# Weight splitting moved from GpSimd to VectorE, narrowing without a clamp, and a later check of the exponents

## The chip, the cores and the metric

One Trainium2 chip, one core. The metric is the device time of the slowest core (here the only one) in microseconds, for one execution of the whole program. Engines: PE (TensorE, with PEld for its weight loads), DVE (VectorE), ACT (ScalarE), POOL (GpSimd) and SP, whose queue issues most DMAs.

## The reference, cut to what matters

Three layers over 3072 tokens of 384 numbers: a recurrent attention, a layer of eight experts with a skip, and a gated layer. The last layer's weights come as 64-bit words (w_gate, w_val, w_out are float64).

```python
def _moe_ref(x, w_skip, w_gate, w1, w2):
    ...
        h = np.maximum(xc[mask] @ w1[e], 0.0)
        y[mask] = gate_w[mask, None] * (h @ w2[e])
    out[do_compute] = xc + y

def _moe2_ref(x, w_gate, w_val, w_out, rms_g):
    rms = np.sqrt(np.mean(x * x, axis=-1, keepdims=True) + 1e-06)
    xn = x / rms * rms_g
    g = xn @ w_gate
    silu = g * (1.0 / (1.0 + np.exp(-g)))
    val = xn @ w_val
    return (silu * val @ w_out).astype(np.float32)
```

w_gate and w_val have 384 x 1536 numbers, w_out 1536 x 384.

## The kernel before, in words

The program runs as one stream of three parts. The order of the instructions on each engine is fixed when the program is built: the build goes through the code in order, takes that order as priority, and places each instruction by a time model of its own. Each engine then works through its own list in that fixed order, and waits at an instruction whose inputs, or whose output buffer, are not ready. So an instruction that waits also holds all that stands behind it on its engine.

**Attention (0 to some 175 us of the profile)**: 24 tiles of 128 tokens, then routing: every token's row is scattered to a slot of its expert.

**Experts (to some 337 us)**: for each of 8 experts, `expert(e)` loads its 256 rows transposed, multiplies by w1 (`products`, line 993), takes relu over as a high and a low half (`relu`, hh on ACT at line 996, hl on DVE at 997) and multiplies by w2 (line 1040). All numbers that PE sees are split in two fp16 halves, hi and lo, and each product is three matmuls (hi hi, hi lo, lo hi). Beside the main loop run side jobs, as generators that are advanced by `steps`, a few steps after each piece of the main loop: `prep1` and `prep2` load and split the weights of an expert three ahead (`split`, lines 390 and 391); `place`, `first` and `middle` take rows of x, form the mean of squares and its inverse root (`square`, lines 444 to 458), and either scatter the normalised row to the buffer xnd (line 477) or transpose it into xnT (line 498).

**The gated layer (the rest)**: six blocks of 512 tokens. `up` makes, for one of 12 slices of 128 columns, the products pwg and pwv (line 846, 9 matmuls each), takes silu of pwg (sg, ACT, line 850), multiplies by pwv (hf, DVE, 852), and splits hf in gh (ACT, 855) and gl (DVE, 856). `down` multiplies these by w_out into four sums po (line 869, 12 matmuls). Blocks 0 and 1 run as one `pair`: all their `up` steps first, alternating, over four pairs of PSUM banks; then the `down` steps. Blocks 2 to 5 run by `block`, where `down` of slice m-1 follows `up` of slice m, over two pairs of banks. `later` brings in a later block's rows, by transposing DMAs on SP's queue.

Before `up` can use slice m it needs the weights of piece m // 2: `prep_in` for w_gate and w_val (6 pieces each of 384 x 256), `prep_out` for w_out (6 of 256 x 384). Each loads a piece as pairs of 32-bit words into a staging tile st (768 KB, four of them) and narrows each 64-bit float to a 32-bit one in `narrow`: the absolute value of the high word on ACT (line 190), a clamp to the range of exponents that the bit trick can take (DVE, 192), shift and mask (193), then sign (195) and low bits (197), all on DVE over 768 columns. The clamp lets a number outside that range show as a too small or too large one. For w_gate and w_val, `prep_in` then scales by rms_g on ACT (three instructions, line 409), casts to the hi half on ACT (414), and subtracts on POOL for the lo half (416). The narrowed tile fb has two buffers.

At the end, `bounds` (lines 916 to 949) gathers checks on ranges, with two small matmuls, and `last` makes a flag of them; if it is set, the program runs a slow general version instead. It is not set here.

Of the kernel before, what the change touches and what calls it, by code (L numbers as in the profile page):

```python
# [34 lines left out]
NPRE = 0  # L35
POOL_LO = True
WB = 3
# [8 lines left out]
N4 = 2  # L46
N5 = 1
HB = 24
FB = 2
# [34 lines left out]
def fused_kernel(ctx, tc, q, k, v, f, w_skip, w_gate, w1, w2, g_gate, g_val, g_out, rms_g, out, dbg=None):  # L84
# [48 lines left out]
    cnt = keep.tile([128, 2 * E + 1], F16, name="cnt")  # L133
    osum = keep.tile([128, NT], F32, name="osum")
    big = keep.tile([128, 2 + 2 * E + 3], F32, name="big")

# [49 lines left out]

    def narrow(o, lo, hi):


        nc.scalar.activation(out=o.bitcast(F32), in_=hi.bitcast(F32), func=AF.Abs)  # L190
        yield
        nc.vector.tensor_scalar(out=o.bitcast(F32), in0=o.bitcast(F32), scalar1=2.0 ** -15 * 1.125, scalar2=2.0 ** 16 * 1.9375, op0=ALU.max, op1=ALU.min)
        nc.vector.tensor_scalar(out=o, in0=o, scalar1=3, scalar2=0x3FFFFFFF, op0=ALU.logical_shift_left, op1=ALU.bitwise_and)
        yield
        nc.vector.scalar_tensor_tensor(out=o, in0=hi, scalar=-0x40000000, in1=o, op0=ALU.bitwise_and, op1=ALU.bitwise_or)
        yield
        nc.vector.scalar_tensor_tensor(out=o, in0=lo, scalar=29, in1=o, op0=ALU.logical_shift_right, op1=ALU.bitwise_or)
        yield
# [195 lines left out]
    def raw(src, n, wide):  # L394
        st = stg.tile([128, n, wide, 2], I32, tag="st", name="st64")
        load(st, src)
        yield
        fb = stg.tile([128, n, wide], I32, tag="fb", name="fb", bufs=FB)
        yield from narrow(fb, st[:, :, :, 0], st[:, :, :, 1])
        return fb.bitcast(F32)  # L400

    def prep_in(nm, p):
        src = (g_gate if nm == "wg" else g_val).bitcast(I32)
        wide = F2 // 6
        w = yield from raw(src[:, 2 * p * wide:2 * (p + 1) * wide].rearrange("(k p) (f t) -> p k f t", p=128, t=2), KD, wide)
        hi, lo = gT[nm][p]
# [15 lines left out]
    def prep_out(p):  # L422
        src = g_out.bitcast(I32)
        w = yield from raw(src[p * 256:(p + 1) * 256, :].rearrange("(k p) (d t) -> p k d t", p=128, t=2), 2, DM)
        yield from split(oT[p][0], oT[p][1], w, SO, 1)
        if p == 0:
            top(big[:, 2 + 2 * E + 2:3 + 2 * E + 2], oT[0][0][:, 0, 0:64])
# [12 lines left out]
    def square(xr, idx, y=None):  # L440
# [9 lines left out]
        m = nk.tile([128, 3], F32, tag="m2", name="m2", bufs=4)  # L450
        nc.scalar.activation(out=junk, in_=x2, func=AF.Square, accum_out=m[:, 0:1])
        nc.gpsimd.tensor_scalar(out=m[:, 1:2], in0=m[:, 0:1], scalar1=1.0 / DM, scalar2=1e-6 * SX * SX, op0=ALU.mult, op1=ALU.add)
        nc.gpsimd.tensor_tensor(out=m[:, 2:3], in0=m[:, 1:2], in1=mhalf[:, 0:1], op=ALU.pow)
# [8 lines left out]
    def place(xr, idx, y=None):  # L462
# [3 lines left out]
        if y is None:  # L466
            ms = m[:, 0:1]
        else:
            junk = nk.tile([128, DM], F32, tag="junk", name="junk", bufs=1)
            m3 = nk.tile([128, 1], F32, tag="m3", name="m3")  # L470
            nc.scalar.activation(out=junk, in_=parts(xr)[:, 0, :], func=AF.Square, accum_out=m3)
            ms = m3
# [358 lines left out]

    hs2 = {}

    def up(blk, m, b0):
# [20 lines left out]
        nc.scalar.copy(out=hh, in_=hf)  # L855
        nc.vector.tensor_tensor(out=hl, in0=hf, in1=hh, op=ALU.subtract)  # L856
        hs2[blk, m] = hh, hl
# [57 lines left out]
    def bounds():  # L915
        NBIG = 2 + 2 * E + 3
        NC = 3 + NBIG
        NA = NC + 2 * E + 1
        bad = keep.tile([128, NC], F32, name="bad")
        vio = keep.tile([128, 4], F32, name="vio")  # L920
        tot = keep.tile([1, NA + NT], F32, name="tot")
# [7 lines left out]
        worst(1, ex_sum, ALU.is_le, EXPSUM, ALU.max)  # L929
        worst(2, ms_x, ALU.is_ge, 1.0, ALU.min)  # L930
        nc.vector.tensor_scalar(out=bad[:, 3:NC], in0=big, scalar1=TINY, scalar2=None, op0=ALU.is_ge)
        pt = ps.tile([128, 512], F32, **bank(3), name="tot")
# [12 lines left out]

        beyond(0, 3, 127.5)
        beyond(3, NC, 0.5)
        beyond(NC, NC + E, LOW, CAP)
# [150 lines left out]
    with m1x:  # L1099
        for e in range(E):  # L1100
            need("a", e)
            need("e", e)
            run(expert(e), N2)
            if e + WB < E:
                add(prep1(e + WB), ("a", e + WB))
                add(prep2(e + WB), ("e", e + WB))
            if e < MID:
                add(middle(e), ("mid", e), 1)
            if 2 <= e < 6:
                for t in (0, 1):  # L1110
                    a = 2 * (e - 2) + t
                    add(first(a // NB, a % NB), ("b", a // NB), 1)
# [10 lines left out]
    for e in range(E):  # L1123
        need("y", e)
    later(2)
    for blk in range(2, NT // NB):
        if blk == NT // NB - 1:
            checks = bounds()
        for m, _ in enumerate(block(blk)):
            if m == 4 and blk + 1 < NT // NB:  # L1130
                later(blk + 1)

    fctx.close()
# [38 lines left out]
```

## Time and profile before

| | us |
|---|---|
| median of 3 runs | 774.69 (773.26 to 774.88) |
| profiled execution, its own time | 774.52 |
| its span | 772.8 |
| PE busy | 719.5 (93% of the span) |
| DVE busy | 417.7 (54%) |
| ACT busy | 362.7 (47%) |
| POOL busy | 216.1 (28%) |

The span is what the profile covers, 1.7 us less than the execution's time. Busy shares are means over three parts that differ; the rows further down are by stretch. The mean granted clock of PE was 0.977 of full speed.

### The profile page before, as it was taken

To read this page: it belongs to the slowest core of one execution; us is meant where nothing else is said; L and a number is where in the kernel's file an instruction comes from. 1 tells how busy PE (TensorE), PEld (TensorE's weight loads), DVE (VectorE), ACT (ScalarE), POOL (GpSimd) and SP (SyncE) were. 2 spreads that over 40 slices of the span, in tenths; PEclk is the share of its full clock that TensorE was granted. 3 is DMA by queue.
4 is the path that set the end of the run, shared out by engine and by line. 5 is a ranking of instruction groups with operands and counts; after the bars stand their busy time and mean duration, and the time that the engine had idled before them with its cause. 6 is when DMAs were issued, how large, how long until landed. Compare 5 with 4: busy or idle time off the path is not lost.

```text
span 772.8 us, 14043 instructions
## 1 busy us (share of the span) xinstructions
PE 719.5 (93%) x5452; PEld 442.8 (57%) x5452; DVE 417.7 (54%) x879; ACT 362.7 (47%) x803; POOL 216.1 (28%) x286
## 2 busy tenths in 40 slices
PE   8999798995999888769999999999999999999995
PEld 5788687784776655534444566455455455555443
DVE  2788386885688888999999700222222222222230
ACT  5887477643577667778766410222312222123131
POOL 5221742442165565677320010200100020002002
PEclk9999899997999999999999999999999999999998
DMA  9999887844778998754332400100200030001001
GB/s 153 178 198 198 209 160 182 231 142 131 217 250 241 265 263 259 237 154 150 110 123 82 82 22 20 42 1 1 62 20 1 1 83 0 1 1 42 1 0 46
DMA packets 166459, 88.10 MB, mean 114 GB/s; under 512 B 137432, under 2 KB 151048, under 8 KB 166384
## 3 DMA queue, kind: packets, MB, share of 16 engines
q1 hardware_dynamic: 161904, 74.44, 39.9%
q0 software_dynamic: 4480, 12.67, 4.5%
q8 instruction: 45, 0.74, 0.4%
q14 instruction: 30, 0.25, 0.1%
HBM read 64.18 MB, written 16.24 MB: 104 GB/s over the span
## 4 chain that ended last, share of the span: by engine, by line
PE 67%; DVE 9%; DMA 8%; ACT 5%; POOL 4%; issue 4%; SPq 2%; POOLq 0%; ACTq 0%; DVEq 0%
PE po L869 18%; PE pwv L846 18%; PE pwg L846 18%; DMA st<-in_moe_w_dram 3%; PE py L641 2%; DMA xnd<-xn,at 2%; PE sc L625 2%; DVE w2l L391 2%; SPq L557 1%; PE py L636 1%; DVE w1l L391 1%; PE ptq L607 1%; DVE xn L458 1%; DVE hl L997 1%; DMA st<-in_moe_w_gate_dram 1%
## 5 line engine op out<-in xcount | busy, mean ns | idle before, releaser
L852 DVE SCALAR_TENSOR_TENSOR hf<-pwv,sg 128x512 f32<-128x512 f32 x72 | 49.5, 689 | 181.4 <-PE pwv L846 181.4
L877 POOL DMA_INDIRECT out_dram<-ot,ids x24 | 23.7, 988 | 336.8 <-ACT ot L876 332.3
L846 PE MATMUL pwg<-xnT,wgh 128*128 128x512 f16 x432 | 106.3, 382 | 7.5 <-ACT sg L850 7.5
L846 PE MATMUL pwv<-xnT,wvh 128*128 128x512 f16 x432 | 105.6, 379 | 0.0
L855 ACT CAST gh<-hf 128x512 f16<-128x512 f32 x72 | 44.3, 615 | 108.5 <-DVE hf L852 108.3
L869 PE MATMUL po<-wol,gh 128*128 128x384 f16 x288 | 93.7, 326 | 0.0
L869 PE MATMUL po<-woh,gh 128*128 128x384 f16 x288 | 93.7, 326 | 0.0
L869 PE MATMUL po<-woh,gl 128*128 128x384 f16 x288 | 93.4, 326 | 0.0
L850 ACT ACTIVATE sg<-pwg 128x512 f32<-128x512 f32 x72 | 42.5, 593 | 101.4 <-PE pwg L846 101.4
L869 PEld LDWEIGHTS <-gh 128*128 128x128 f16 x576 | 56.4, 98 | 41.8
L846 PEld LDWEIGHTS <-wgh 128*128 128x128 f16 x432 | 42.5, 98 | 55.4 <-issue 8.9
L856 DVE TENSOR_TENSOR gl<-hf,gh 128x512 f16<-128x512 f32 x72 | 52.6, 731 | 35.4 <-ACT gh L855 35.4
L846 PEld LDWEIGHTS <-wvh 128*128 128x128 f16 x432 | 42.3, 98 | 50.4 <-issue 0.3
L993 PE MATMUL ph<-exT,w1h 128*128 128x256 f16 (+1 forms) x384 | 57.3, 276 | 8.5 <-DMA exT<-xs 8.5
L846 PE MATMUL pwg<-xnT,wgl 128*128 128x512 f16 x216 | 59.3, 381 | 0.0
L846 PE MATMUL pwv<-xnT,wvl 128*128 128x512 f16 x216 | 58.7, 379 | 0.0
L993 PEld LDWEIGHTS <-w1h 128*128 128x128 f16 x432 | 40.6, 101 | 19.9 <-DMA exT<-xs 8.6
L1040 PE MATMUL ey<-w2h,hh 128*128 128x384 f16 x112 | 37.0, 331 | 7.1 <-ACT hh L996 7.1
L588 POOL TENSOR_TENSOR qs<-q,ep 128x384 f32<-128x384 f32 x24 | 26.8, 1117 | 56.3 <-ACT ep L584 38.5
L876 ACT ACTIVATE ot<-po 128x384 f32<-128x384 f32 x24 | 11.6, 489 | 58.2 <-PE po L869 50.9
L869 PEld LDWEIGHTS <-gl 128*128 128x128 f16 x288 | 28.2, 98 | 18.6
L1040 PE MATMUL ey<-w2h,hl 128*128 128x384 f16 x112 | 31.4, 332 | 7.1 <-DVE hl L997 5.2
(203 smaller groups left out, 1396.0 us busy)
## 6 DMA issues: line engine op xcount, KB each, us to landing
st<-in_moe_w_dram SPq DMA_DIRECT2D x32, 768.0 KB, 6.3
f<-in_f_logit_dram SPq DMA_DIRECT2D x24, 192.0 KB, 4.6
q<-in_q_dram SPq DMA_DIRECT2D x24, 192.0 KB, 4.0
k<-in_k_dram SPq DMA_DIRECT2D x24, 192.0 KB, 4.6
v<-in_v_dram SPq DMA_DIRECT2D x24, 192.0 KB, 4.4
st<-in_moe_w_gate_dram SPq DMA_DIRECT2D x6, 768.0 KB, 4.6
st<-in_moe_w_val_dram SPq DMA_DIRECT2D x6, 768.0 KB, 4.6
st<-in_moe_w_out_dram SPq DMA_DIRECT2D x6, 768.0 KB, 4.3
```

The source lines that it names most:

```text
L391: nc.vector.scalar_tensor_tensor(out=lo[:, :, sl], in0=src[:, :, sl], scalar=scale, in1=hi[:, :, sl], op0=ALU.mult, op1=ALU.subtract)
L588: nc.gpsimd.tensor_tensor(out=qs[:, :, 0:D], in0=ins["q"], in1=ep, op=ALU.mult)
L625: nc.tensor.matmul(scs[r][:, j, :], lhsT=T["k"][64 * r:64 * r + 64, j, :], rhs=T["q"][64 * r:64 * r + 64, j, :], start=True, stop=True)
L846: nc.tensor.matmul(p, lhsT=w, rhs=x, start=(j == 0), stop=(j == len(terms) - 1))
L850: nc.scalar.activation(out=sg, in_=pg, func=AF.Silu, scale=1.0 / SG)
L852: nc.vector.scalar_tensor_tensor(out=hf, in0=pv, scalar=SH / SG, in1=sg, op0=ALU.mult, op1=ALU.mult)
L855: nc.scalar.copy(out=hh, in_=hf)
L856: nc.vector.tensor_tensor(out=hl, in0=hf, in1=hh, op=ALU.subtract)
L869: nc.tensor.matmul(po[t], lhsT=a[:, sl], rhs=w, start=(m == 0 and j == 0), stop=(m == KF2 - 1 and j == 2))
L877: sc = nc.gpsimd.indirect_dma_start(out=out, out_offset=bass.IndirectOffsetOnAxis(ap=at[:, t:t + 1].bitcast(U32), axis=0), in_=ot, in_offs ...
L993: nc.tensor.matmul(out[:, i, :], lhsT=a, rhs=r, start=(j == 0), stop=(j == len(terms) - 1))
L1040: nc.tensor.matmul(py[t], lhsT=a[:, sl], rhs=w[:, m, :], start=(m == 0 and j == 0), stop=(m == KF - 1 and j == 2))
```

## The change

- `prep_in`: ACT's scaling writes the hi half directly (the cast is gone), and the lo half is made on DVE, by three instructions of 256 columns that scale and subtract, in place of one on POOL of 768.
- `narrow` without the clamp for these weights: neither the absolute value on ACT nor the clamp on DVE; the shift reads the raw high words in the staging tile. The side job of a piece of w_out is one step shorter for it; that of w_gate or w_val two, since the subtraction's own step is gone too.
- The range of exponents, which the clamp covered, is checked by `ranges`: each of the 18 pieces is loaded a second time, its exponent fields are shifted out, and their maximum and minimum are kept (DVE). It runs as a side job in the blocks from 2 on, two steps after each slice, behind gl on DVE, and must be over when the last block starts. `bounds` has two more columns.
- In `square` and `place` the mean's factor goes into ACT's scale, and the addition of epsilon moves from POOL to DVE.
- The table of functions that silu needs is loaded behind the last relu of expert 0, and not where silu is first met.

```diff
-POOL_LO = True
+POOL_LO = False
...
+N6 = 2
...
-    def narrow(o, lo, hi):
-        nc.scalar.activation(out=o.bitcast(F32), in_=hi.bitcast(F32), func=AF.Abs)
-        yield
-        nc.vector.tensor_scalar(out=o.bitcast(F32), in0=o.bitcast(F32), scalar1=2.0 ** -15 * 1.125, scalar2=2.0 ** 16 * 1.9375, op0=ALU.max, op1=ALU.min)
-        nc.vector.tensor_scalar(out=o, in0=o, scalar1=3, scalar2=0x3FFFFFFF, op0=ALU.logical_shift_left, op1=ALU.bitwise_and)
+    def narrow(o, lo, hi, clamp=True):
+        src = hi
+        if clamp:
+            nc.scalar.activation(out=o.bitcast(F32), in_=hi.bitcast(F32), func=AF.Abs)
+            yield
+            nc.vector.tensor_scalar(out=o.bitcast(F32), in0=o.bitcast(F32), scalar1=2.0 ** -15 * 1.125, scalar2=2.0 ** 16 * 1.9375, op0=ALU.max, op1=ALU.min)
+            src = o
+        nc.vector.tensor_scalar(out=o, in0=src, scalar1=3, scalar2=0x3FFFFFFF, op0=ALU.logical_shift_left, op1=ALU.bitwise_and)
...
-        yield from narrow(fb, st[:, :, :, 0], st[:, :, :, 1])
+        yield from narrow(fb, st[:, :, :, 0], st[:, :, :, 1], clamp=False)
...
+    def ranges():
+        j = 0
+        for source, n, wide in [in_source(nm, p) for nm in ("wg", "wv") for p in range(6)] + [out_source(p) for p in range(6)]:
+            st = stg.tile([128, n, wide, 2], I32, tag="st", name="st64")
+            nc.sync.dma_start(out=st, in_=source)
+            yield
+            fb = stg.tile([128, n, wide], I32, tag="fb", name="fb", bufs=FB)
+            nc.vector.tensor_scalar(out=fb, in0=st[:, :, :, 1], scalar1=20, scalar2=0x7FF, op0=ALU.logical_shift_right, op1=ALU.bitwise_and)
+            yield
+            nc.vector.tensor_reduce(out=expo[:, 0, j:j + 1], in_=fb, axis=AX.XY, op=ALU.max)
+            yield
+            nc.vector.tensor_reduce(out=expo[:, 1, j:j + 1], in_=fb, axis=AX.XY, op=ALU.min)
+            yield
+            j += 1
...
-        nc.scalar.activation(out=junk, in_=x2, func=AF.Square, accum_out=m[:, 0:1])
-        nc.gpsimd.tensor_scalar(out=m[:, 1:2], in0=m[:, 0:1], scalar1=1.0 / DM, scalar2=1e-6 * SX * SX, op0=ALU.mult, op1=ALU.add)
+        nc.scalar.activation(out=junk, in_=x2, func=AF.Square, scale=DM ** -0.5, accum_out=m[:, 0:1])
+        nc.vector.tensor_scalar(out=m[:, 1:2], in0=m[:, 0:1], scalar1=1e-6 * SX * SX, scalar2=None, op0=ALU.add)
...
-        nc.vector.tensor_tensor(out=hl, in0=hf, in1=hh, op=ALU.subtract)
+        gated.append(nc.vector.tensor_tensor(out=hl, in0=hf, in1=hh, op=ALU.subtract).ins)
...
+        worst(3, expo[:, 0], ALU.is_le, 1150.0, ALU.max)
+        worst(4, expo[:, 1], ALU.is_ge, 897.0, ALU.min)
...
+            if e == 0:
+                with tc.issue_after(pins[-1][0]):
+                    nc.scalar.preload_act_table_set("silu_and_others")
...
+    add(ranges(), ("ranges",))
     for blk in range(2, NT // NB):
         if blk == NT // NB - 1:
+            need("ranges")
             checks = bounds()
         for m, _ in enumerate(block(blk)):
             if m == 4 and blk + 1 < NT // NB:
                 later(blk + 1)
+            with tc.issue_after(gated[-1]):
+                steps(N6)
```

With `POOL_LO = False` the branch of `prep_in` that was not taken before is taken:

```python
            else:
                nc.scalar.activation(out=hi[:, j, :], in_=w[:, j, :], func=AF.Copy, scale=gsc[:, j:j + 1])
                nc.vector.scalar_tensor_tensor(out=lo[:, j, :], in0=w[:, j, :], scalar=gsc[:, j:j + 1], in1=hi[:, j, :], op0=ALU.mult, op1=ALU.subtract)
```

`issue_after(x)` places what stands in it behind x in the list of x's engine, without a wait.

## Rows read from the trace of the kernel before

**Rows 1.** Busy time by stretch of the span. Columns: the stretch in us and its length; then for PE, PEld (weight loads), DVE (VectorE), ACT (ScalarE) and POOL (GpSimd) the busy us in it and (x instructions); then the granted TensorE clock as a share of full speed, the DMA share and GB/s.
```profile
280.00:300.00 20.00, 16.38 (x112) 11.27 (x111) 13.76 (x33) 12.23 (x32) 9.88 (x12) 0.91 0.92 231
...
320.00:340.00 20.00, 17.31 (x107) 10.33 (x108) 19.92 (x32) 13.73 (x33) 16.97 (x15) 1.00 0.77 253
340.00:345.00 5.00, 0.00 (x0) 0.00 (x0) 4.93 (x12) 2.75 (x6) 3.46 (x5) 0.90 0.16 18
...
370.00:436.00 66.00, 66.00 (x307) 29.91 (x306) 63.40 (x85) 40.95 (x70) 10.62 (x6) 1.00 0.30 90
...
484.00:560.00 76.00, 76.00 (x389) 37.95 (x388) 18.06 (x27) 18.40 (x37) 5.61 (x6) 1.00 0.10 26
...
705.00:773.00 68.00, 58.89 (x307) 29.76 (x305) 14.39 (x23) 13.76 (x27) 3.88 (x4) 0.96 0.04 14
```

**Rows 2.** Instructions of PE in order of time at the start of the last part. Columns: start us, length us (of the whole group), engine, line, operation, output<-inputs, shape, how many; in brackets the idle time before and what ended it.
```profile
339.09 0.81 PE L846 MATMUL pwg<-xnT,wgl 128*128 128x512 f16 x3
347.44 2.72 PE L846 MATMUL pwg<-xnT,wgh 128*128 128x512 f16 x6 [7.53 <-ACT sg L850]
349.95 1.26 PE L846 MATMUL pwg<-xnT,wgl 128*128 128x512 f16 x3
...
352.99 1.46 PE L846 MATMUL pwg<-xnT,wgh 128*128 128x512 f16 x6
```

**Rows 3.** The chain of waits that ended last, in order of time, between 311 and 348 us. Columns: start us, us that the piece adds to the chain, engine, tile and line.
```profile
317.97 0.86 DVE w2l L391
...
320.65 0.47 DVE fb L192
...
321.64 0.33 DVE hl L997
...
328.94 0.88 DVE fb L197
...
338.52 1.60 POOL wgl L416
...
340.14 0.92 ACT fb L190
...
342.12 0.07 DVE at L476
...
345.49 1.28 ACT L850
...
346.79 0.61 ACT sg L850
```

**Rows 4.** Instructions of DVE in order of time before the first gate product is taken over, columns as in rows 2.
```profile
324.30 1.99 DVE L458 SCALAR_TENSOR_TENSOR xn<-x,m,xn 128x384 f16<-128x384 f32 x1
...
334.23 1.54 DVE L458 SCALAR_TENSOR_TENSOR xn<-x,m,xn 128x384 f16<-128x384 f32 x1
...
336.67 3.87 DVE L192 TENSOR_SCALAR fb<-fb 128x768 f32<-128x768 f32 x1
...
344.21 0.62 DVE L458 SCALAR_TENSOR_TENSOR xn<-x,m,xn 128x384 f16<-128x384 f32 x1
...
348.26 0.68 DVE L852 SCALAR_TENSOR_TENSOR hf<-pwv,sg 128x512 f32<-128x512 f32 x1
```

**Rows 5.** Instructions of POOL in order of time in the same stretch: the three lo-half subtractions that ran in it.
```profile
323.91 1.97 POOL L416 TENSOR_TENSOR wgl<-fb,wgh 128x768 f16<-128x768 f32 x1
...
333.52 1.84 POOL L416 TENSOR_TENSOR wvl<-fb,wvh 128x768 f16<-128x768 f32 x1
...
338.47 1.64 POOL L416 TENSOR_TENSOR wgl<-fb,wgh 128x768 f16<-128x768 f32 x1
```

**Rows 6.** Groups of instructions by line of DVE between 311 and 348 us. Columns: line, engine, operation, output<-input, shapes, how many | busy us, mean ns of one | idle us before.
```profile
L192 DVE TENSOR_SCALAR fb<-fb 128x768 f32<-128x768 f32 x5 | 6.3, 1256 | 0.2 <-ACT fb L190 0.2
...
L193 DVE TENSOR_SCALAR fb<-fb 128x768 int32<-128x768 int32 x5 | 4.2, 841 | 0.1
```

**Rows 7.** Instructions of ACT in order of time around the end of expert 0, columns as in rows 2.
```profile
201.24 0.30 ACT L996 ACTIVATE eah<-ph 128x160 f16<-128x160 f32 x1 [1.29 <-PE ph L993]
...
204.17 0.38 ACT L996 ACTIVATE hh<-ph 128x256 f16<-128x256 f32 x1 [1.17 <-PE ph L993]
```

**Rows 8.** Groups of instructions by line over the whole span. Columns: line, engine, operation, output<-input, shapes, how many | busy us, mean ns of one | idle us of the engine just before them and what ended it.
```profile
L458 DVE SCALAR_TENSOR_TENSOR xn<-x,m,xn 128x384 f16<-128x384 f32 x30 | 24.1, 805 | 6.1 <-ACT xn L457 6.0
...
L452 POOL TENSOR_SCALAR m<-m 128x1 f32<-128x1 f32 x30 | 13.8, 459 | 22.6 <-ACT junk L451 21.4
...
L146 DVE TENSOR_REDUCE big<-w2h 128x1 f32<-128x64 f16 x8 | 1.7, 210 | 0.0
...
L925 DVE TENSOR_REDUCE vio<-dec 128x1 f32<-128x192 f32 x1 | 0.4, 353 | 0.0
```

**Rows 9.** Instructions of DVE in order of time in a late block (block 2), columns as in rows 2.
```profile
498.57 0.69 DVE L856 TENSOR_TENSOR gl<-hf,gh 128x512 f16<-128x512 f32 x1 [0.68 <-ACT gh L855]
503.02 0.69 DVE L852 SCALAR_TENSOR_TENSOR hf<-pwv,sg 128x512 f32<-128x512 f32 x1 [3.77 <-PE pwv L846]
504.40 0.69 DVE L856 TENSOR_TENSOR gl<-hf,gh 128x512 f16<-128x512 f32 x1 [0.68 <-ACT gh L855]
```

**Rows 10.** The first product of the same block step that needs the tile gl written at 498.57, on PE, columns as in rows 2.
```profile
503.08 0.33 PE L869 MATMUL po<-woh,gl 128*128 128x384 f16 x1
```

**Rows 11.** DMA issues of one line over the whole span. Columns: output<-input, queue, kind, how many, KB each, median us from issue to landing.
```profile
st<-in_moe_w_out_dram SPq DMA_DIRECT2D x6, 768.0 KB, 4.3
```

More of the change, by code (lines that the diff above doesn't have):

```diff
@@ L134, in fused_kernel @@
     osum = keep.tile([128, NT], F32, name="osum")
+    expo = keep.tile([128, 2, 18], F32, name="expo")
     big = keep.tile([128, 2 + 2 * E + 3], F32, name="big")
@@ L398, in raw, with in_source, out_source, prep_in @@
         fb = stg.tile([128, n, wide], I32, tag="fb", name="fb", bufs=FB)
-        yield from narrow(fb, st[:, :, :, 0], st[:, :, :, 1])
+        yield from narrow(fb, st[:, :, :, 0], st[:, :, :, 1], clamp=False)
         return fb.bitcast(F32)
-    def prep_in(nm, p):
+    def in_source(nm, p):
         src = (g_gate if nm == "wg" else g_val).bitcast(I32)
         wide = F2 // 6
-        w = yield from raw(src[:, 2 * p * wide:2 * (p + 1) * wide].rearrange("(k p) (f t) -> p k f t", p=128, t=2), KD, wide)
+        return src[:, 2 * p * wide:2 * (p + 1) * wide].rearrange("(k p) (f t) -> p k f t", p=128, t=2), KD, wide
+    def out_source(p):
+        return g_out.bitcast(I32)[p * 256:(p + 1) * 256, :].rearrange("(k p) (d t) -> p k d t", p=128, t=2), 2, DM
+    def ranges():
[12 more added lines that the diff above has]
+            j += 1
+    def prep_in(nm, p):
+        w = yield from raw(*in_source(nm, p))
         hi, lo = gT[nm][p]
@@ L422, in prep_out @@
     def prep_out(p):
-        src = g_out.bitcast(I32)
-        w = yield from raw(src[p * 256:(p + 1) * 256, :].rearrange("(k p) (d t) -> p k d t", p=128, t=2), 2, DM)
+        w = yield from raw(*out_source(p))
         yield from split(oT[p][0], oT[p][1], w, SO, 1)
@@ L470, in place @@
             m3 = nk.tile([128, 1], F32, tag="m3", name="m3")
-            nc.scalar.activation(out=junk, in_=parts(xr)[:, 0, :], func=AF.Square, accum_out=m3)
+            nc.scalar.activation(out=junk, in_=parts(xr)[:, 0, :], func=AF.Square, scale=DM ** -0.5, accum_out=m3)
             ms = m3
@@ L832, in fused_kernel @@
     hs2 = {}
+    gated = []
     def up(blk, m, b0):
@@ L916, in bounds @@
         NBIG = 2 + 2 * E + 3
-        NC = 3 + NBIG
+        NC = 5 + NBIG
         NA = NC + 2 * E + 1
         bad = keep.tile([128, NC], F32, name="bad")
-        vio = keep.tile([128, 4], F32, name="vio")
+        vio = keep.tile([128, 5], F32, name="vio")
         tot = keep.tile([1, NA + NT], F32, name="tot")
@@ L929, in bounds @@
         worst(1, ex_sum, ALU.is_le, EXPSUM, ALU.max)
-        worst(2, ms_x, ALU.is_ge, 1.0, ALU.min)
-        nc.vector.tensor_scalar(out=bad[:, 3:NC], in0=big, scalar1=TINY, scalar2=None, op0=ALU.is_ge)
+        worst(2, ms_x, ALU.is_ge, 1.0 / DM, ALU.min)
+        worst(3, expo[:, 0], ALU.is_le, 1150.0, ALU.max)
+        worst(4, expo[:, 1], ALU.is_ge, 897.0, ALU.min)
+        nc.vector.tensor_scalar(out=bad[:, 5:NC], in0=big, scalar1=TINY, scalar2=None, op0=ALU.is_ge)
         pt = ps.tile([128, 512], F32, **bank(3), name="tot")
@@ L944, in beyond @@
                 nc.vector.tensor_scalar(out=o, in0=o, scalar1=(most - mid) ** 2, scalar2=None, op0=ALU.is_gt)
-        beyond(0, 3, 127.5)
-        beyond(3, NC, 0.5)
+        beyond(0, 5, 127.5)
+        beyond(5, NC, 0.5)
         beyond(NC, NC + E, LOW, CAP)
```

## The prediction

> **What bounds the kernel now.** I read the busy time by stretch first. From 370 us on PE has no idle time: 66.00 of 66.00 us and 76.00 of 76.00, and the last stretch lacks only the end of the program [rows 1]. Nothing that frees VectorE, ScalarE or GpSimd can shorten that part; it can only be disturbed. So the time can be won before it, where PE is short of work: 16.38 of 20.00 us at 280 to 300, 17.31 of 20.00 at 320 to 340, and nothing at all from 340 to 345 [rows 1]. In those last two stretches DVE is busy for 19.92 of 20.00 and 4.93 of 5.00 us, while ACT has 13.73 and 2.75. DVE is what runs late there.
>
> The order of time on PE shows the largest single loss: after the gate product at 339.09 it stands still for 7.53 us until the first sigmoid product sg is done, and comes back at half the pace: six products take 2.72 us against 1.46 at 352.99, the next three 1.26 against 0.81, so another 1.71 us are gone [rows 2]; 0.81 us is the full-pace length of three, as at 339.09. The granted clock in the stretch of standstill is already 0.90 [rows 1].
>
> The chain of waits behind that sg runs through DVE (w2l, fb, hl), then POOL wgl 1.60, ACT fb 0.92, DVE again, an ACT piece of 1.28 at line 850 that is no computation but the load of the function table, and sg itself [rows 3]. sg's input is a product that ran before the standstill; sg stands in ACT's fixed order behind work that waits for DVE.
>
> Why DVE is late shows when its long instructions are laid beside POOL's. xn<-x,m,xn takes 0.62 us at 344.21, but 1.99 at 324.30 and 1.54 at 334.23; a clamp takes 3.87 at 336.67 [rows 4]. POOL's lo-half subtractions run from 323.91 to 325.88, from 333.52 to 335.36 and from 338.47 to 340.11 [rows 5], and each slow DVE instruction ends about 0.4 us after such a one. I read this as DVE being held for as long as the POOL instruction runs.
>
> **The change, part by part.** The sum is made against the profiled execution, 774.52 us, which is 0.17 below the median of 774.69; only the stretch from 311 to 348 us carries terms, since it ends at the hand-off that PE waits for.
>
> Lo halves leave POOL. Held time that ends: 1.99 - 0.62 = 1.37, 1.54 - 0.62 = 0.92, and the 1.64 of the third subtraction, which lies whole inside the 3.87 us clamp [rows 4, 5]: 3.93 us less for DVE. In exchange DVE makes three subtractions of 256 columns per source. The nearest row is hl, also two inputs and 256 columns: 0.33 us of chain [rows 3]. Five sources are narrowed on DVE in this stretch [rows 6]; the fifth ends just before hf at 348.26, so its lo halves come after it. Four sources by three by 0.33 is 3.96 us more.
>
> No clamp. Five clamps at 0.47 us unheld [rows 3, 6]: 2.35 us less.
>
> The shift now reads the raw words, 8 bytes apart, and not a packed tile. The trace has no such instruction. Below: 0.47, as the clamp, the same kind with one input [rows 3]; above: 0.88, as fb at 328.94, which reads with that step [rows 3]. But w2l at 317.97 reads packed and takes 0.86 for as many columns: what the 0.88 pays for is the second input, not the step. I take 0.47, so nothing; the upper end is 5 x 0.41 = 2.05 us.
>
> The Trainium skill, Advanced Engine Details and Errata, section VectorE Performance Modes, points the same way for the one thing that the rows leave open: it lists for the two-port double rate that both tensors lie in SBUF and that their outer dimensions match, and no unit step. By it the sum below stands at -3.1; by the row with the same step it would be -1.05. No run so far shows this instruction.
>
> Sigmoid table. 1.28 us stand directly ahead of sg [rows 3]; moved behind expert 0's last relu at 201.24 they fall where ACT has 1.17 us of idle time before its next hh [rows 7]. So 1.28 less here, and 0.11 there, which I leave out. Without that cover it costs 1.28.
>
> Abs and the cast from ACT. ACT waits for DVE rather than the other way, so I take nothing; if the Abs at 340.14 truly ends last, 0.92 us less [rows 3].
>
> Mean of squares: the small step moves from POOL (0.459 us on average) to DVE [rows 8]. A one-column DVE step adds 0.07 to the chain [rows 3]; seven or so tiles pass in this stretch, 0.5 us more. But on POOL it waited 21.4 us in all for ACT's square [rows 8], and on DVE every later instruction queues behind it: hl and xn, for which PE and the scatters wait. The nearest DVE instruction that waits for ACT in the same way, xn, idles 6.0 us over 30, 0.2 each [rows 8]. That bounds it at 0 and 7 x 0.27 = 1.9 us; I take 0.5, since DVE arrives late at nearly everything here.
>
> Second load and exponent check. 18 loads on SP's queue, 18 shifts and 36 reductions on DVE, in blocks 2 to 4. A reduction of 768 columns is not in the trace: 64 columns take 210 ns, 192 take 353 [rows 8], so 1.12 ns a column and about 1.0 us. Two passes, at most 2.0 us, follow each gl, where DVE idles 3.77 us [rows 9]. If they were late, hf would be too, but gl is over at 499.26 and its first product is at 503.08 [rows 9, 10]: 3.8 us more. So 7.6 us of cover per step against 2.0: nothing. If the shift must wait for its load, that wait may be up to 5.6 us; a load of this size lands in 4.3 [rows 11], and four staging tiles let SP issue ahead. On SP the loads stand among the transposes for blocks 3 to 5; these are wanted a whole block later (a block's stretch is 76 us [rows 1]), so a load waiting for a staging tile holds up nothing. The extra columns in the final check are one product and a few steps before the end.
>
> Sum: -3.93 - 1.28 - 2.35 + 3.96 + 0.5 = -3.1, that is 771.4 us. The standstill on PE shrinks to some 4.4 us, and the slow restart stays. With the bounds: -3.1 - 0.5 - 0.92 = -4.5 at best; -3.1 + 2.05 + 1.4 + 1.28 = +1.6 at worst: its own range is 770.0 to 776.1.
>
> **The rivals.** *The standstill closes.* Every engine's order is planned anew. With less ACT work ahead of it, and no sources that look free to do early, sg may come to stand right behind its product; then 7.53 + 1.71 = 9.24 us go: 765.3. For it: sg's own input is ready at once. Against: other hand-offs come at the same time, hf at 348.26 among them [rows 4].
>
> *It does what it says, off the path.* DVE is relieved of 6.3 us and given 4.5; if PE's restart hangs on a transfer or a bank instead, only the table load is left, 773.2, or nothing.
>
> *The hold turns round (slower).* The new lo halves read two tiles on DVE and may hold POOL as POOL held DVE. POOL's sums and powers feed xn, which DVE needs; then the 3.93 us come back as waits, and if the shift is at its upper end, it is -3.1 + 3.93 + 2.05 = +2.9: 777.4. It decides once less than 0.8 us of the 3.93 is left and the shift costs 0.88. The Trainium skill, SBUF — State Buffer, section SBUF: two separate sides, says just this: whichever of the two starts first has the shared ports for its whole instruction, and a VectorE instruction with two SBUF inputs counts. The trace agrees for one direction, with the 3.87 us above.
>
> *The check breaks its cover (slower).* If loads land later than 5.6 us after the gl they follow, each of 18 costs the excess: at 6.3 us 0.7 x 18 = 12.6 us, 787.1. Against it stands the 4.3 us and an almost idle DMA (share 0.10) [rows 1, 11].
>
> **How the numbers follow.** Forecast 0.42, standstill closes 0.20, off the path 0.18, hold turns round 0.15, check 0.05. About 0.2%, 1.5 us, is what a measurement can tell from no change. Faster: 0.38 of the forecast, all of the second, 0.04 of the third: 0.62. Same: 0.04, 0.14 and 0.02 of the fourth: 0.20. Slower: 0.13 and 0.05: 0.18. The range leaves out the last two: 765.0 to 776.5; the forecast's own is above.
>
> **What would show it.** Right: no POOL subtraction of 768 columns, no DVE xn above 1 us where such a one ran, no table load after 340, PE's standstill before the second part 3 to 5 us, and PE still without idle time in blocks 2 to 4 with DVE near twice as busy. The shift's row decides between 0.47 and 0.88. Wrong: a standstill of 7 us or more, or one gone; DVE waiting for ACT's square; PE waiting for gh or gl in blocks 2 to 4.

## The result, and the profile of the changed kernel

The change made the kernel slower: 777.54 us median (776.32 to 781.51) against 773.26 us (769.36 to 774.88) of the kernel before on the same chip, ratio 1.0074, 95% interval 1.0053 to 1.0095 (the ratio is the recorded estimate from all executions; the quotient of the two medians would be 1.0055). The forecast was 771.4, and its range ended at 776.5. The profiled execution took 776.53 us with a span of 774.8.

The stretches of the changed kernel, in the form of [rows 1] (start:end, length, busy time of PE, PEld, DVE, ACT, POOL, granted clock of PE, DMA share, GB/s); the first line is of the kernel before:

```profile
230.00:260.00 30.00, 27.12 (x200) 18.49 (x198) 24.74 (x52) 21.12 (x50) 17.11 (x22) 1.00 0.80 229
```
```profile
230.00:260.00 30.00, 24.15 (x151) 15.78 (x150) 18.81 (x49) 18.56 (x43) 14.85 (x15) 0.85 0.66 205
320.00:340.00 20.00, 17.09 (x100) 10.53 (x101) 20.00 (x49) 9.28 (x25) 8.94 (x9) 0.91 0.69 219
340.00:345.00 5.00, 2.79 (x9) 1.10 (x9) 5.00 (x10) 3.11 (x8) 2.58 (x4) 0.81 0.49 155
345.00:350.00 5.00, 2.49 (x7) 0.75 (x6) 5.00 (x10) 0.81 (x2) 2.05 (x1) 0.50 0.71 205
484.00:560.00 76.00, 76.00 (x391) 38.07 (x389) 30.91 (x45) 18.52 (x40) 5.17 (x6) 1.00 0.33 94
```

The late blocks are as forecast: at 484 to 560 DVE works 30.91 us where it had 18.06 [rows 1], the DMA share is 0.33, and PE has no gap. The standstill ahead of the gated layer has become smaller too, as forecast. What the prediction did not look at is the stretch from 230 to 260, among the experts: PE is busy 24.15 us at a granted clock of 0.85, and in the kernel before 27.12 us at 1.00.

PE of the changed kernel in order of time, four of the places where it waited (start, length, engine, line, operation, output<-inputs, shape, count, idle time before and what ended it):

```profile
229.28 0.34 PE L1069 MATMUL ey<-w2h,hh 128*128 128x384 f16 x1 [1.97 <-ACT hh L1025]
237.30 0.82 PE L1069 MATMUL ey<-w2h,hl 128*128 128x384 f16 x2 [2.15 <-DVE hl L1026]
342.21 1.87 PE L873 MATMUL pwg<-xnT,wgh 128*128 128x512 f16 x6 [2.44 <-ACT sg L877]
347.87 2.72 PE L873 MATMUL pwg<-xnT,wgh 128*128 128x512 f16 x6 [2.51 <-DVE x L472]
```

Ahead of the gated layer 7.53 us of standstill [rows 2] have become 2.44 + 2.51, with six products in 2.72 us after the second: the 4.4 us and the slow restart of the forecast. But hl comes late for the experts. Why shows when DVE and POOL are laid side by side around that wait:

```profile
227.98 0.96 DVE L396 SCALAR_TENSOR_TENSOR w2l<-st,w2h 128x768 f16<-128x768 f32 x1 [3.25 <-ACT w2h L395]
228.85 0.15 DVE L478 TENSOR_SCALAR m<-m 128x1 f32<-128x1 f32 x1
228.99 0.62 DVE L484 SCALAR_TENSOR_TENSOR xn<-x,m,xn 128x384 f16<-128x384 f32 x1
236.55 0.17 DVE L500 COPY xn<-xr 128x4 f32<-128x4 f32 x1 [4.47 <-issue]
236.82 0.42 DVE L1026 SCALAR_TENSOR_TENSOR hl<-ph,hh 128x256 f16<-128x256 f32 x1
```

```profile
229.08 0.94 POOL L479 TENSOR_TENSOR m<-m,mhalf 128x1 f32<-128x1 f32 x1 [4.00 <-DVE m L478]
230.20 1.66 POOL L503 DMA_INDIRECT xnd<-xn,at  x1 [0.18 <-issue]
232.97 0.99 POOL L503 DMA_INDIRECT xnd<-xn,at  x1 [0.17 <-issue]
```

DVE's head stands 3.25 us at w2l, whose high part ACT makes late, because ACT itself has waited 4.20 us for the load of these weights. Behind it is the small step m (0.15 us). POOL's pow has waited 4.00 us for it, and behind that pow, in POOL's list, stand two scatters of xn. They go out at 230.20 and 232.97. DVE, meanwhile, comes to a copy into one of the two xn buffers; the program's semaphores make that copy wait for the scatter that reads the buffer, and it waits 4.47 us (the row says "issue", so that it is the scatter is read from the program; a2 below bears it out). Behind the copy stands hl, and PE waits 2.15 us for it. The small step has tied DVE and POOL into a ring.

These waits are not the whole price. Below is the stretch from the first expert product to the 217th gated one, the same products each time, in the kernel before, the changed one, a1 and b1 of the next section:

```profile
176.95:389.87 212.92, 182.66 (x1253) 116.73 (x1251) 180.09 (x351) 144.49 (x318) 114.45 (x126) 0.95 0.72 208
```
```profile
174.60:391.60 217.00, 189.24 (x1255) 121.01 (x1252) 178.58 (x413) 131.66 (x303) 91.33 (x87) 0.91 0.71 213
```
```profile
180.90:387.40 206.50, 182.80 (x1255) 117.68 (x1253) 174.45 (x376) 130.67 (x301) 98.12 (x117) 0.96 0.74 218
```
```profile
176.97:404.18 227.21, 186.00 (x1254) 118.58 (x1252) 174.47 (x380) 145.58 (x318) 106.11 (x97) 0.93 0.67 196
```

In the changed kernel PE idles 27.8 us here, in the kernel before 30.3: it waits less in all. What is longer is its busy time for the same products, 189.2 us against 182.7, at a granted clock of 0.91 against 0.95. Against a1 both are longer, idle time by 4.1 us and busy time by 6.4; b1 loses mostly by waiting, 41.2 us. So the loss is partly waits, and partly products that run slower at the lower clock.

### The profile page after: what moved, and what is told of

Its sections match the earlier page's. It is cut to its first block, busy times and chain, and to the rows that moved or that the text cites. A ratio compares the mean times of both kernels' runs of the same rounds, so it can differ in the third digit from the quotient of the medians.

```text
span 774.8 us, 14115 instructions
## 1 busy us (share of the span) xinstructions
PE 724.6 (94%) x5452; PEld 446.1 (58%) x5452; DVE 445.0 (57%) x985; ACT 340.9 (44%) x773; POOL 187.7 (24%) x244
## 4 chain that ended last, share of the span: by engine, by line
PE 65%; DVE 12%; DMA 9%; issue 6%; ACT 4%; POOL 3%; POOLq 0%; SPq 0%; ACTq 0%; DVEq 0%
PE po L896 18%; PE pwg L873 16%; PE pwv L873 16%; DMA xnd<-xn,at 4%; PE py L667 2%; PE sc L651 2%; PE py L662 2%; DVE w2l L396 1%; PE ptq L633 1%; POOL m L479 1%; DMA xnT<-xn 1%; DVE w1l L396 1%; PE ptk L633 1%; DMA f<-in_f_logit_dram 1%; DVE xn L484 1%
## 5 line engine op out<-in xcount | busy, mean ns | idle before, releaser
L883 DVE TENSOR_TENSOR gl<-hf,gh 128x512 f16<-128x512 f32 x72 | 50.6, 704 | 36.6 <-ACT gh L882 36.6
L1022 PE MATMUL ph<-exT,w1h 128*128 128x256 f16 (+1 forms) x384 | 60.8, 284 | 8.6 <-DMA exT<-xs 8.6
L1069 PE MATMUL ey<-w2h,hl 128*128 128x384 f16 x112 | 32.0, 346 | 10.4 <-DVE hl L1026 10.4
```

The costliest lines, as they stand in the source:

```text
L883: gated.append(nc.vector.tensor_tensor(out=hl, in0=hf, in1=hh, op=ALU.subtract).ins)
L1022: nc.tensor.matmul(out[:, i, :], lhsT=a, rhs=r, start=(j == 0), stop=(j == len(terms) - 1))
L1069: nc.tensor.matmul(py[t], lhsT=a[:, sl], rhs=w[:, m, :], start=(m == 0 and j == 0), stop=(m == KF - 1 and j == 2))
```

## The experiments

All ratios are to the kernel before on the same chip. Three numbers read from the traces stand beside each. A: us from the first to the 433rd expert product, the stretch of the ring above. B: us from the first to the 109th gated product, the hand-over to the gated layer. P: mean us from the end of ACT's sum of squares to the start of POOL's pow, for the 26 to 29 tiles between 200 and 350 us. A to P are of one profiled execution each (b2's was its slowest, 779.36 us against a median of 773.87). From the 217th gated product to the last `down` product each of these kernels takes 373.5 us, with the exponent check or without it.

| kernel | ratio, 95% interval | A | B | P |
|---|---|---|---|---|
| before | 1 | 93.0 | 34.7 | 1.52 |
| changed | 1.0074, 1.0053 to 1.0095 | 101.3 | 34.6 | 2.05 |
| a1: changed, epsilon on POOL | 0.9936, 0.991 to 0.9962 | 94.4 | 27.2 | 1.28 |
| b1: before, epsilon on DVE | 1.0126, 1.0101 to 1.0152 | 102.9 | 43.7 | 2.23 |
| b2: before, lo halves on DVE | 0.9957, 0.9934 to 0.998 | 96.7 | 31.9 | 1.36 |
| a2: changed, 3 xn | 1.0111, 1.0081 to 1.0141 | 100.2 | 35.3 | 2.01 |
| c1: changed, 3 xn, 4 at | 1.0031, 1.0014 to 1.0049 | 94.5 | 36.4 | 1.73 |
| c2: a1 with an idle DVE step | 0.9913, 0.9887 to 0.9939 | 94.1 | 25.6 | 1.10 |
| c5: changed, epsilon on ACT | 0.9934, 0.9909 to 0.9959 | 96.1 | 26.2 | 1.21 |
| e1: changed, old order on POOL | 1.0047, 1.0026 to 1.0067 | 93.0 | 38.7 | 2.09 |
| f1: e1 with the buffers of c1 | 1.0005, 0.9979 to 1.003 | 92.7 | 36.0 | 1.88 |
| g1: c5 with the buffers of c1 | 0.9928, 0.9901 to 0.9955 | 95.5 | 26.8 | 1.18 |
| d1: a1 with the buffers of c1 | 0.9877, 0.9851 to 0.9902 | 94.2 | 26.6 | 1.03 |
| f2: before with the buffers of c1 | 1.0026, 1.0005 to 1.0047 | 92.5 | 33.3 | 1.34 |
| c4: a1 without the check | 0.9918, 0.9895 to 0.9942 | 92.8 | 27.5 | 1.30 |
| d2: a1 without the early table load | 0.9936, 0.9913 to 0.9959 | 95.8 | 27.1 | 1.24 |
| d3: a1 with lo halves on POOL | 1.0055, 1.0031 to 1.0078 | 94.3 | 34.8 | 1.56 |
| d4: before without clamps | 1.0079, 1.0048 to 1.0109 | 93.2 | 36.1 | 1.63 |

### Whose loss is it: the small step alone

a1 takes one line back and b1 makes it alone (both with the factor 1/DM and its limit):

```diff
-        nc.vector.tensor_scalar(out=m[:, 1:2], in0=m[:, 0:1], scalar1=1e-6 * SX * SX, ...)
+        nc.gpsimd.tensor_scalar(out=m[:, 1:2], in0=m[:, 0:1], scalar1=1.0 / DM, ...)
```

> The changed kernel with one part undone: the addition of epsilon and the factor 1/384 are back on POOL, as in the kernel before. Theory T1 (the small step on DVE's queue makes POOL's power, the scatter to xnd and, through the two xn buffers, DVE's own copy into xn late): the 9.0 us in which DVE stood at that copy are gone, PE reaches expert 6 some 5 us earlier than in the changed kernel, and the time is 769 to 773 us, 4 us or more under the changed kernel. Rival T2 (late loads of expert weights, or another planned order, cause the loss): 776 to 779, no difference from the changed kernel.

> The kernel before with one part of the change alone: the factor goes into ACT's square and the addition of epsilon to DVE. T1: slower than before by 4 to 8 us (777 to 781), with POOL's power waiting for DVE's small step for some 15 us in all, and DVE waiting at the copy into xn. T2: within 1.5 us of the kernel before.

Both came out on the theory's side, b1 with more than the 4 to 8 us that it allowed: the step costs 1.38% on the changed kernel (1.0074 less 0.9936, some 10.7 us) and 1.26% on the old one (9.8 us). All the rest of the change together is a gain of 0.64%, some 5 us. B shows where: 34.6 us falls to 27.2.

### The instruction or the hand-over of work

c2 keeps the DVE instruction beside a1's on POOL, but lets it write a column that nobody reads; c5 puts the step on ACT:

```diff
+        nc.vector.tensor_scalar(out=m[:, 3:4], in0=m[:, 0:1], scalar1=1e-6 * SX * SX, ...)     # c2
+        nc.scalar.activation(out=m[:, 1:2], in_=m[:, 0:1], func=AF.Copy, bias=1e-6 * SX * SX)  # c5
```

> The changed kernel with epsilon added on GpSimd as before, and VectorE's 128x1 step kept beside it, writing a column of m that nobody reads: the same instruction on the same engine behind the same sum of ScalarE, but GpSimd's pow no longer waits for it. Theory, the loss is the coupling of GpSimd's queue to VectorE's: as the version without the step, ratio 0.991 to 0.997. Rival, the loss is the step's own place in VectorE's queue (its time and its wait for ScalarE's sum): ratio 1.001 to 1.008.

> The changed kernel with the small step (adding epsilon to the mean of squares) on ScalarE, the engine that has just made the sum, and not on VectorE; GpSimd keeps only the pow. Theory, what costs is that GpSimd waits for a third queue: here it waits for ScalarE as before the change, ratio 0.990 to 0.997. Rival, a step more on any engine ahead of the pow delays it as much: ratio 1.003 to 1.010.

Both as the theory had it. The DVE instruction by itself costs nothing that these runs show; that POOL waits for it does. P agrees: 1.03 to 1.63 us where the step that pow waits for stands on POOL or ACT, 1.73 to 2.23 where it stands on DVE. Within the first group it does not follow the ratio. c5 also bears on the rival that loads of expert weights come late: ACT waits 9.1 us for those of w2 between 200 and 340 us, nearly as in the changed kernel (10.1; 5.1 in the kernel before), and c5 is as fast as a1. Late loads alone are not the loss.

### How the tie costs: order and buffers

a2 has the first of these lines, c1 both:

```diff
-        xn = nk.tile([128, ROW], F32, tag="xn", name="xn")
+        xn = nk.tile([128, ROW], F32, tag="xn", name="xn", bufs=3)
-        at = nk.tile([128, 1], I32, tag="at", name="at")
+        at = nk.tile([128, 1], I32, tag="at", name="at", bufs=4)
```

> The changed kernel with three buffers of xn in place of two, so that the copy into xn need not wait for the last scatter but one. T1: the wait of DVE at the copy into xn falls from 9.0 us to under 2, POOL's power still waits for DVE's small step, and the time falls by 3 to 6 us, to 771 to 775. T2: no more than 1.5 us of difference from the changed kernel.

This expectation failed: a2 is no faster than the changed kernel (1.0111, and the intervals overlap). With three xn buffers the copy no longer waits, but the next write that the same scatter releases does:

```profile
238.83 0.15 DVE L502 TENSOR_SCALAR at<-xr 128x1 int32<-128x1 f32 x1 [3.79 <-DMA xnd<-xn,at]
```

So c1 opens both. The second cure, e1, came from the instruction lists: in the kernel before, POOL has the pow of a tile ahead of the next tile's sum x; in the changed one the build's time model puts the sum first and both pows behind it. On DVE, xn of the first tile then stands behind w2l of the next weights. e1 ties the sum behind the last pow, by order only:

```diff
-            nc.gpsimd.tensor_tensor(out=x2, in0=x2, in1=parts(xr)[:, 1, :], op=ALU.add)
+            with tc.issue_after(pows[-1]) if pows else ExitStack():
+                nc.gpsimd.tensor_tensor(out=x2, in0=x2, in1=parts(xr)[:, 1, :], op=ALU.add)
```

> The changed kernel with three buffers for xn and four for at, so that no copy on VectorE waits any more for a scatter of xn that has not landed. With three xn buffers alone the wait moved from the copy into xn (9.0 and 3.5 us) to the write of at (8.6 us). Theory, the loop closes through the scatter: with both legs open VectorE's waits on xnd and xnT in 200 to 350 fall below 2 us in all, TensorE's waits for hl halve, and the ratio comes to 0.993 to 0.999. Rival, the lateness lies on GpSimd before the scatter (its pow waits for VectorE's small step 16 us in all) and does not need the way back: the waits on VectorE go, TensorE's waits for hl, hh and x stay over 15 us, and the ratio stays at 1.004 to 1.012.

> The changed kernel, small step on VectorE as changed, with one edge of order more: GpSimd's sum x (second instruction of a tile that comes from an expert) is issued behind the last pow traced before it. In the kernel before, GpSimd's list has the pow of one tile ahead of the next tile's sum; in the changed one the build's time model puts the sum first and both pows behind it, and on VectorE xn of the first tile behind w2l of the next weights. The edge brings the old order back, on GpSimd and so on the engines that follow. Theory, the loss is that order: ratio 0.992 to 0.998, and no wait of VectorE at the copy into xn above 3 us. Rival, the crossing itself (GpSimd waits for VectorE's step in whatever order): 1.003 to 1.011.

> The changed kernel, small step on VectorE, with both cures at once: the edge of order on GpSimd (the next tile's sum behind the last pow) and three xn and four at buffers. In the version with the edge alone the stall of 8.38 us ahead of the gated layer hangs, by the chain of waits, on a write of at that waits for a scatter. Theory, list order and the way back through the buffers are together the whole loss: ratio 0.987 to 0.993, no stall over 2 us ahead of the gated layer. Rival, the crossing from VectorE to GpSimd costs by itself where VectorE is full: 0.997 to 1.004, with a stall of 3 us or more there.

> The kernel before with three xn and four at buffers and nothing else. Theory, there GpSimd is not late, and VectorE's waits for the scatter (1.8 and 2.4 us) lie beside other work: 0.998 to 1.002. Rival, the buffers are worth what they gave on the version with epsilon on GpSimd (0.9936 to 0.9877) in any kernel: 0.992 to 0.996.

c1 falls between its two expectations, just under the rival's band: VectorE's waits for the scatter are gone and TensorE's for hl are 1.6 us (10.4 in the changed kernel), as the theory had it, but not the time. e1 lies in its rival's band, and so does f1. A and B tell why: each cure alone brings A back to about the old length (94.5 and 93.0 from 101.3), but A weighs less than it seems. Of the 8.3 us by which it is longer in the changed kernel than before, 4.4 come back by the first gated product, which follows the 433rd product by 57.6 us and not by 62.0. B stays at 36.4, 38.7 and 36.0. Ahead of the gated layer PE stands still in each of them; the first two lines are c1's, the third e1's, the last two f1's:

```profile
340.72 2.72 PE L873 MATMUL pwg<-xnT,wgh 128*128 128x512 f16 x6 [3.51 <-ACT sg L877]
350.10 2.11 PE L873 MATMUL pwg<-xnT,wgh 128*128 128x512 f16 x6 [3.77 <-DMA xnT<-xn]
```
```profile
350.30 2.72 PE L876 MATMUL pwg<-xnT,wgh 128*128 128x512 f16 x6 [8.38 <-DVE x L474]
```
```profile
342.65 2.54 PE L876 MATMUL pwg<-xnT,wgh 128*128 128x512 f16 x6 [2.76 <-ACT sg L880]
352.33 2.00 PE L876 MATMUL pwg<-xnT,wgh 128*128 128x512 f16 x6 [3.95 <-DMA xnT<-xn]
```

Just ahead of that place the changed kernel's DVE has no idle time (20.00 of 20.00 us), so a step put there comes late by what is queued. f1's tile whose transposed copy PE waits for, first its sum on ACT, then the step on DVE, then POOL's pow, and last xn:

```profile
340.68 0.19 ACT L480 ACTIVATION_READ_ACCUMULATOR junk<-x 128x1 f32 x1
```
```profile
343.02 0.14 DVE L481 TENSOR_SCALAR m<-m 128x1 f32<-128x1 f32 x1
348.05 0.61 DVE L487 SCALAR_TENSOR_TENSOR xn<-x,m,xn 128x384 f16<-128x384 f32 x1
```
```profile
343.24 1.38 POOL L482 TENSOR_TENSOR m<-m,mhalf 128x1 f32<-128x1 f32 x1 [1.77 <-DVE ms_x L525]
```

The sum is there at 340.87, pow starts at 343.24, 2.37 us later, and xn, which in DVE's list stands behind other work, follows at 348.05, 3.43 us after pow's end. In d1, with the same buffers and epsilon on POOL, pow follows its sum by 0.36 us (331.97 to 332.33), and PE's wait is

```profile
340.48 1.46 PE L873 MATMUL pwg<-xnT,wgh 128*128 128x512 f16 x6 [0.80 <-DMA xnT<-xn]
```

at full pace afterwards. f2 shows that the buffers are no gain by themselves: 1.0026, a little above its theory's band and far from the rival's. In its profiled execution they do shorten the way from the first expert product to the 109th gated one, by 3.6 us, but then a second standstill takes back more than that:

```profile
374.53 2.72 PE L846 MATMUL pwg<-xnT,wgh 128*128 128x512 f16 x6 [4.75 <-ACT sg L850]
```

> The changed kernel with three xn and four at buffers and the small step on ScalarE in place of VectorE; it differs from the version with the same buffers and the step on VectorE (1.0031) by the engine of that one step. Theory, what is left is the step's place in the queue of the engine that is full: 0.986 to 0.992, no stall over 2 us ahead of the gated layer. Rival, GpSimd pays for a step on any other engine: 0.997 to 1.004.

g1 differs from c1 by the engine of the step alone and goes from 1.0031 to 0.9928, a little above the theory's band and clear of the rival's; B falls from 36.4 to 26.8. With the buffers open the step on DVE costs 1.03% against ACT (c1, g1) and 1.54% against POOL (c1, d1); with two buffers of xn it was 1.40% (c5) and 1.38% (a1). So most of the loss is the step's place in the queue of the engine that is full, and not the way back through the buffers. How much of it is the wait, and how much the order that the build derives from it on all engines, these runs don't separate: e1 and f1 restore POOL's order in the experts' stretch, not every engine's list.

### The other parts of the change

b2 and d3 set POOL_LO alone; d4 takes the clamp out of the kernel before for the gated layer's weights; d2 drops the early load of the table, c4 the check (the exponents are not looked at); d1 adds c1's buffers to a1:

```diff
-POOL_LO = True
+POOL_LO = False                                                    # b2; d3 the other way round, in a1
-        yield from narrow(fb, st[:, :, :, 0], st[:, :, :, 1])
+        yield from narrow(fb, st[:, :, :, 0], st[:, :, :, 1], clamp=False)   # d4
-                    nc.scalar.preload_act_table_set("silu_and_others")       # d2, in a1
-    add(ranges(), ("ranges",))
+    nc.gpsimd.memset(expo, 1000.0)                                 # c4, in a1
```

> The kernel before with the lo halves of gate and value weights on DVE alone (clamp and all else as before). By the terms of the prediction: holds of DVE under POOL's subtraction end (3.93 us less), lo halves cost 3.96 more, so 0 to 1 us of difference, 772 to 775, and PE's standstill before the gated layer stays at 6 to 8 us. If the lo halves were what made the changed kernel slower, it is 776 or more.

> The kernel before without the clamps of the gated layer's weights (Abs on ScalarE and max/min on VectorE), nothing else of the change; the exponents are not looked at. The prediction's term is -2.35 us: ratio 0.995 to 0.998. Rival, with the lo halves on GpSimd a source that VectorE finishes sooner only waits for GpSimd, whose subtractions then hold VectorE at other places: 0.999 to 1.006.

> The changed kernel with epsilon and the lo halves both on GpSimd, so that of the change only the clamps, the table load and the check are left. The prediction's terms for these are -2.35 and -1.28 us: ratio 0.994 to 0.9965. Rival, the standstill ahead of the second gate product is set by the lo halves held on GpSimd and VectorE alike (alone, moved to VectorE, they gave 0.9957): then it stays, 0.998 to 1.001.

> The changed kernel with epsilon on GpSimd and without the early load of the function table; the table is then loaded ahead of the first sigmoid product, as before the change. The prediction's term is 1.28 us: ratio 0.993 to 0.9965 (0.0017 above the version with it, which stood at 0.9936 and, with an idle step, 0.9913). Rival, the load is hidden now that TensorE comes back for another reason (a transfer): no difference, 0.990 to 0.993.

> The changed kernel with epsilon on GpSimd and without the check of the exponents in blocks 2 to 5: the second load of gate, value and output weights and its 54 VectorE instructions are left out, the maxima and minima are set to 1000. The prediction's step puts the check at nothing: ratio within 0.002 of that with the check (0.9936). Rival, loads and VectorE work break the cover somewhere: 0.987 to 0.991.

> The changed kernel with epsilon on GpSimd and three xn and four at buffers. With epsilon on GpSimd VectorE still waits 1.9 us at the copy into xn and 2.5 us at at. Theory, those are not where TensorE's time goes: ratio as with two buffers, 0.991 to 0.995. Rival, they hold hl as they did in the changed kernel: 0.986 to 0.990.

The lo halves alone gain 0.43% (b2), more than the 0 to 1 us that had been expected, and PE's longest wait ahead of the gated layer is 4.15 us, not 6 to 8. The clamps alone (d4) do not give 2.35 us, they cost 0.79%, some 6 us: the rival's case, and more. d3, the same with the table load and the check, is 0.55% slower, which neither side had. A source that DVE finishes sooner is waiting for POOL, as d4's chain of waits shows (start, us in the chain, what), a stretch in which nearly every piece is POOL's (pieces under 0.1 us are left out; ahead of it the chain has 5.39 us for a load of an expert's rows, so a transfer has a share in it that these runs don't separate):

```profile
365.71 0.91 POOL x L450
366.61 2.05 POOL wvl L419
368.67 1.59 POOL x L450
370.34 0.52 POOL m L455
370.93 1.37 POOL m L456
372.39 0.92 POOL m L455
373.40 1.28 POOL m L456
374.70 0.62 ACT xn L460
375.31 0.72 ACT wgh L417
376.04 0.50 ACT sg L853
376.58 3.02 PE pwg L849 x9
```

It ends in a second standstill of PE, 2.58 us before 376.58, which the kernel before does not have: that kernel takes 23.3 us from the 109th to the 217th gated product, d3 and d4 take 27.7. f2, which has its clamps, takes 31.1, with POOL's subtractions (4.09 and 2.16 us) in the chain ahead of the wait shown above. So it is not the clamps as such; in both kernels the chain runs through POOL. a1 and d3 differ by the lo halves alone and lie 1.19% apart, nearly three times what the lo halves gave on the old kernel. Once the subtractions are off POOL, leaving out the clamps no longer costs; that it then pays is not shown: b2 has the clamps and no check, d2 the check and no clamps, and their intervals overlap (0.9957 and 0.9936).

d2 stays inconclusive: 0.9936 is in the band of the 1.28 us, but also a1's own number. The trace speaks for the rival: in a1 and d2 PE waits 1.44 and 1.39 us for xnT at that place, not for sg, and B is 27.2 and 27.1. c4 is within 0.002 of a1, with overlapping intervals, and the late blocks last equally long: the check costs nothing that these runs show. d1 beats both kernels: 0.9877, 767.51 us against 777.19. That is the rival's band; d2, measured beside it, had 771.94, so with epsilon on POOL the buffers do pay on the changed kernel. With epsilon on ACT they show no gain (c5 0.9934, g1 0.9928), and why the two differ is open.

## Why the prediction was wrong, step by step

**The mean of squares: the step that failed.** The prediction put +0.5 us on it, with 1.9 as its upper bound; measured alone it is 9.8 us on the old kernel and 10.7 on the new. It had said that on DVE every later instruction queues behind it. The delay runs the other way: the step queues behind whatever DVE waits for, and POOL's pow and two scatters queue behind the step. The bound came from how long DVE would wait for ACT; in the changed kernel DVE's waits for that sum don't appear among its longest, and POOL's pow waits 35.0 us in the whole program for DVE, where POOL waited 21.4 us for ACT [rows 8]. pow reads only m; the row also names ms_x, the step right behind m on DVE:

```profile
L479 POOL TENSOR_TENSOR m<-m,mhalf 128x1 f32<-128x1 f32 x30 | 28.5, 959 | 35.0 <-DVE m L478 18.4 <-DVE ms_x L499 11.7 <-DVE ms_x L522 4.8
```

And it was costed in the stretch from 311 to 348 alone, seven or so of 30 tiles; the ring closes at 229 and again at 253, where the copy into xn waits 4.57 us more. There was no term either for what later waits do to PE's clock outside the one restart: PE's busy time grew by 6.6 us for the same products. Of the prediction's own signs of being right, those on the standstill and on the late blocks came true while the time went the other way, since none of them looked at the experts.

**The standstill.** Right in size (4.95 us against 4.4), with the slow restart. But it gave no time: B is 34.6 us against 34.7, since PE idles 2.6 us less in it and is busy 2.6 us longer. And that was the changed kernel with its tie; without the tie (a1) it is 1.44 us, six products take 1.46, and the rival "the standstill closes" is nearly what happens, though PE then waits for a transfer. Its 765.3 is 0.988 of the time before; a1 came to 0.9936, and that d1 came to 0.9877 is no support, since d1 has more buffers besides.

**Clamps, holds and lo halves.** The terms were added as if independent. Alone, lo halves give -3.3 us and clamps +6.1; a1 has both, with table load and check, and gains 5. Where the stall goes that the clamps free was not asked: POOL was next. A lo half costs 0.40 us from start to start, not 0.33, so 4.8 for the twelve and not 3.96. Holding goes on, by POOL's sums, which the prediction did not count as holding:

```profile
339.38 1.94 DVE L439 SCALAR_TENSOR_TENSOR wvl<-fb,gsc,wvh 128x256 f16<-128x256 f32 x2
```
```profile
340.10 0.93 POOL L470 TENSOR_TENSOR x<-xr 128x384 f32<-128x384 f16 x1
```

**The shift.** Right. It takes 0.54 to 0.58 us with raw words 8 bytes apart, 0.47 from start to start, where the row with the same step would have given 0.88. The reading of the Trainium skill that the prediction weighed (Advanced Engine Details and Errata, VectorE Performance Modes) holds for this instruction.

**Table load.** Its 1.28 us could not be shown as a gain in time: once PE waits for a transfer at that place (d2) they lie off the path. In the changed kernel itself, where PE waits 2.44 us for sg, it was not tried.

**Check of exponents.** Right. A reduction of 768 columns takes 0.94 us (forecast 1.0), two of them 1.88 against 7.6 us of cover:

```profile
506.11 0.69 DVE L883 TENSOR_TENSOR gl<-hf,gh 128x512 f16<-128x512 f32 x1 [0.68 <-ACT gh L882]
506.71 0.94 DVE L425 TENSOR_REDUCE expo<-fb 128x1 f32<-128x768 int32 x1
507.58 0.94 DVE L427 TENSOR_REDUCE expo<-fb 128x1 f32<-128x768 int32 x1
510.56 0.69 DVE L879 SCALAR_TENSOR_TENSOR hf<-pwv,sg 128x512 f32<-128x512 f32 x1 [2.04 <-PE pwv L873]
```

**The slower rival.** "The hold turns round" gave 777.4, and 777.54 was measured, but by another mechanism, so the near hit is luck (as ratios 1.0037 and 1.0074). Of its two conditions the shift failed (0.47 us, not 0.88). POOL is held somewhat longer: its 16 sums x take 1.21 us on average, 1.06 before. But in a1 they take 1.21 too, and a1 is faster than the kernel before.

## What to carry to other kernels

When a small step moves to another engine, price whom it makes wait, not its length: name what stands ahead of it in the new queue, what stands behind its reader, and whether that leads back, in every stretch where the step runs. A second cure that removes one link can move the wait to the next buffer of the same transfer; open them together. And terms for two engines that feed each other are not added: freeing the one can cost time until the other has been freed. Look at PE's busy time as well as its waits: less waiting at a lower clock can still be slower.

## What the runs showed of the hardware

A DVE instruction can last through several POOL instructions in a row. In d4 a shift, 0.55 us elsewhere in the same trace, takes 4.00 us:

```profile
339.21 4.00 DVE L196 TENSOR_SCALAR fb<-st 128x768 int32<-128x768 int32 x1
```
```profile
339.40 0.92 POOL L447 TENSOR_TENSOR x<-xr 128x384 f32<-128x384 f16 x1
340.26 0.93 POOL L450 TENSOR_TENSOR x<-x,exr 128x384 f32<-128x384 f32 x1
341.13 1.65 POOL L419 TENSOR_TENSOR wvl<-fb,wvh 128x768 f16<-128x768 f32 x1
```

It ends 0.43 us after the last of the three, 341.13 + 1.65 = 342.78. The Trainium skill, SBUF — State Buffer, section SBUF: two separate sides, lets one engine hold the other for a whole instruction; here the row is longer than any one of them, as if the three had been one. That DVE was held is read from the lengths and ends; no run takes the three apart. The 3.87 us clamp of [rows 4], from 336.67 to 340.54, is such a case: two sums run on POOL ahead of the subtraction of [rows 5].

```profile
336.74 0.92 POOL L444 TENSOR_TENSOR x<-xr 128x384 f32<-128x384 f16 x1
337.60 0.92 POOL L447 TENSOR_TENSOR x<-x,exr 128x384 f32<-128x384 f32 x1
```

So moving the subtraction off POOL leaves the part of the hold that the sums make.
